# A fused RWKV, dense FFN and expert-choice MoE kernel: one-hot products for the first expert's newest rows, all second products of the last dense block held, an early start of the routing search, and one raw place kept free

## The chip, the core and the metric

The kernel runs on one core of one Trainium2 chip. The metric is device time in microseconds (us), the median of several executions. TensorE (PE) does the matmuls, VectorE (DVE) and ScalarE (ACT) work on tiles, GpSimd (POOL) and SyncE (SP) mostly issue DMAs.

## What is computed

Three parts follow one another, and the third is what matters here:

```python
x = attention(r, k, v, w, u)          # 4 x 768 tokens, 8 heads of 48: x is 3072 x 384
h = x @ w_in                          # 384 -> 2048
x = (h * sigmoid(1.702 * h)) @ w_out  # 2048 -> 384
logits = x @ w_gate                   # 8 experts
order = argsort(-logits.flatten())    # greedy: best (token, expert) pair first,
...                                   # an expert takes cap = 384 tokens, a token goes to one expert
for e in range(8):
    mask = assigned == e
    out[mask] = maximum(x[mask] @ w1[e], 0) @ w2[e]   # 384 -> 1024 -> 384
```

All of it is float32. The dense and expert weights and their inputs are split into a high and a low part (`fp32r`), so that one float32 product is three passes: high by high, high by low, low by high.

## The kernel before

**Tokens.** 3072 tokens are 24 tiles of 128 rows. Eight dense blocks of three tiles (384 tokens) run one after the other. In a block a column `f` (128 of the 2048 hidden units) has a first product `g1` (9 matmuls of 128x384, line 1207), a GELU on ACT with a split by ACT and DVE, and a second product `g2` (three `part`s of 3 matmuls, line 1235, one per tile). The result of a tile goes by ACT (line 1350) into a `cva` tile `x2` and by a DMA of ACT's queue (line 1353) to DRAM as `x2d`.

**The last block.** The routing must know all logits, so the last block makes its logits straight from the hidden columns (`thin_logits`, line 1479, two matmuls per column). Its second products are only needed later. `NIN = 2` columns are multiplied at once, the other 14 are held: 12 (`NHOLD`) in places of the ring `hold`, two in the tiles `gh`. Their 42 `part`s are the list `parts_left`. They are multiplied, tile by tile, while DVE and PE run the search of the first expert.

**Routing.** `Router.route` finds, per expert, which tokens it takes. `best()` takes each token's best open expert and makes a key; the search cuts the key in five rounds (64, 64, 64, 128, 128 steps). A round is a comparison on DVE (line 284), 24 counting matmuls (line 429), a threshold on DVE and one small matmul (line 434). Then come the expert's number `ei` (line 328), ranks, and `slots()`, which makes row numbers `idx` by 24 matmuls (line 492). `ei` lets SP read the expert's weights (line 1621, eight reads of 384 KB into `hold` places); `idx` lets POOL gather the 384 rows of `x2d` by three indirect DMAs (line 1684).

**An expert.** Each raw weight tile is split: ACT makes the high part (line 1640); the low part is made by ACT's negative copy (line 1657) with an accumulating DMA of POOL (line 1665), or, where the planner holds the DMA engines to be behind, by one DVE subtraction (line 1648). The gathered rows are transposed on PE (line 1700), split by ACT (1709) and DVE (1711), and then the eight columns run `g1` and `g2`. The search of the next experts runs between them.

**Who sets the order.** Every engine's program is fixed when the kernel is built. A planner (`Issue`) steps through a clock of its own: chains (generators) yield costs, and where the main line has nothing to do it puts filler matmuls into PE's program: narrow ones (`spin`, line 732, 128x128) or, before the first expert, wide ones (`spin_wide`, line 1783, 128x512), whose results nobody reads. On the chip an engine then runs its list in order and waits only for data.

**Between the last block and the first expert** the gathers wait for the store of the last tile, since they read all of `x2d`; the third raw read of the first expert is held back by a one-element ACT write (line 1617), the fourth by a one-element POOL write (line 1620) that stands behind the gathers.

```python
    sc.until(lambda: "ffn" in EX[0] and ("raw1", 0, 0) in wdone)   # fillers until the first expert can start
```

## Time and profile before

| | us |
|---|---|
| median of 3 executions | 822.85 (821.57 to 823.52) |
| the profiled execution, its own time | 822.38 |
| its span in the profile | 820.4 |
| last held second product ends | 550.4 |
| first matmul of the first expert starts | 564.3 |
| last matmul starts | 811.74 |

Times inside the span count from its start. The profile has one row per group of instructions; a matmul's row shows how long one matmul is in flight, which is longer than the distance at which the next one follows it.

### The profile page before, as it was taken

The numbers are of one execution on the slowest core, as the hardware profiler recorded it, in microseconds if no ns is written. First come the engines' busy times: TensorE is split into PE (matmuls) and PEld (weight loads), VectorE is DVE, ScalarE is ACT, GpSimd is POOL, SyncE is SP. The second block draws the span as 40 slices with busy tenths as digits, with TensorE's granted clock in tenths as the row PEclk, the third lists the DMA queues.
The fourth block names the chain that finished last, engine by engine and source line by source line (L and its number), as shares of the span: only waits on it lengthen the run. The fifth ranks groups of instructions, "written<-read, shape, count | busy, mean of one in ns | idle before, by whom it ended". The sixth has DMA issues, their size and how long they took to land.

```text
span 820.4 us, 17510 instructions
## 1 busy us (share of the span) xinstructions
PE 803.3 (98%) x6608; PEld 756.6 (92%) x6608; DVE 622.8 (76%) x1424; ACT 472.7 (58%) x1178; POOL 140.6 (17%) x188
## 2 busy tenths in 40 slices
PE   8999999999999999999999999999999999999995
PEld 7898999999999999999999999988898988989995
DVE  9977898879879888888879827478888887875310
ACT  5754653575676686686676644214556645576421
POOL 1001001001201101100102000003334443454211
PEclk9999999999999999999999999999999999999999
DMA  9833634412313313303313000028889899989400
GB/s 289 227 114 107 205 117 138 130 28 84 112 32 106 112 27 98 111 23 103 111 26 107 6 12 20 2 80 223 224 222 246 240 262 244 267 226 332 89 30 29
DMA packets 46068, 105.85 MB, mean 129 GB/s; under 512 B 7352, under 2 KB 13344, under 8 KB 45984
## 3 DMA queue, kind: packets, MB, share of 16 engines
q1 hardware_dynamic: 30816, 68.21, 26.5%
q0 software_dynamic: 10416, 29.50, 16.5%
q10 hardware_dynamic: 4752, 7.03, 2.4%
q8 instruction: 51, 0.84, 0.4%
q14 instruction: 33, 0.27, 0.1%
HBM read 73.60 MB, written 10.03 MB: 102 GB/s over the span
## 4 chain that ended last, share of the span: by engine, by line
PE 84%; issue 6%; DMA 5%; DVE 2%; POOL 1%; ACT 1%; SPq 0%; POOLq 0%; ACTq 0%; DVEq 0%
PE g L1207 33%; PE acc L1235 33%; PE s L1071 3%; PE s L1153 3%; PE s L429 2%; DMA cvb<-x2d,idx 2%; PE s L809 2%; PE s L1148 1%; DMA hold<-in_w 1%; DMA nat_v<-in_v 1%; PE s L1088 1%; PE s L1103 1%; PE acc L732 1%; PE s L1479 1%; POOL out L1743 1%
## 5 line engine op out<-in xcount | busy, mean ns | idle before, releaser
L1235 PE MATMUL acc<-wk,gh 128*128 128x384 f32 x1080 | 283.2, 340 | 0.1
L1235 PEld LDWEIGHTS acc<-wk,gh 128*128 128x128 f32 x1080 | 193.3, 188 | 1.6 <-issue 0.6
L1235 PE MATMUL acc<-wk,gl 128*128 128x384 f32 x540 | 181.9, 337 | 0.0
L1207 PE MATMUL g<-xha,wk 128*128 128x384 f32 x576 | 166.1, 340 | 0.0
L1207 PE MATMUL g<-xhb,wk 128*128 128x384 f32 x576 | 164.5, 339 | 0.0
L1282 ACT ACTIVATE cvb<-cvb 128x384 f32<-128x384 f32 x240 | 122.7, 517 | 8.4 <-DVE cvb L1293 7.9
L1253 ACT ACTIVATE g<-g 128x384 f32<-128x384 f32 x128 | 60.9, 476 | 101.1 <-PE g L1207 95.9
L1207 PEld LDWEIGHTS g<-xha,wk 128*128 128x128 f32 x576 | 105.4, 188 | 1.1 <-issue 0.3
L1207 PEld LDWEIGHTS g<-xhb,wk 128*128 128x128 f32 x576 | 105.1, 188 | 0.3
L1235 PEld LDWEIGHTS acc<-wk,gl 128*128 128x128 f32 x540 | 101.4, 188 | 0.0
L1207 PE MATMUL g<-xlb,wk 128*128 128x384 f32 x288 | 97.5, 339 | 0.0
L1207 PE MATMUL g<-xla,wk 128*128 128x384 f32 x288 | 97.2, 338 | 0.0
L1056 POOL TENSOR_SCALAR_AFFINE_SELECT At<-dg 128x512 f32<-128x512 f32 x38 | 35.0, 944 | 361.1 <-DVE dg L1049 273.5
L1259 DVE TENSOR_TENSOR gl<-g,gh 128x384 fp32r<-128x384 f32 x116 | 63.5, 548 | 29.1 <-ACT gh L1256 28.9
L1266 ACT ACTIVATE gh<-g 128x384 fp32r<-128x384 f32 x64 | 31.4, 491 | 88.8 <-PE g L1207 81.5
L1269 DVE SCALAR_TENSOR_TENSOR gl<-g,gh 128x384 fp32r<-128x384 f32 x64 | 35.3, 552 | 43.7 <-ACT gh L1266 43.6
L1293 DVE TENSOR_TENSOR cvb<-cva,raw 128x768 f32<-128x768 f32 x60 | 57.2, 963 | 8.5 <-ACT cva L1350 4.8
L1256 ACT ACTIVATE gh<-g 128x384 fp32r<-128x384 f32 x116 | 56.5, 487 | 6.5 <-ACT cva L1350 2.4
L1640 ACT ACTIVATE wk<-hold 128x768 fp32r<-128x768 f32 x64 | 52.9, 840 | 10.3 <-DMA hold<-in_w 10.3
L1665 POOL DMA_DIRECT2D wk<-hold x51 | 46.4, 1026 | 65.1 <-ACT wk L1657 51.9
L1207 PEld LDWEIGHTS g<-xlb,wk 128*128 128x128 f32 x288 | 54.1, 188 | 0.1
L1207 PEld LDWEIGHTS g<-xla,wk 128*128 128x128 f32 x288 | 54.1, 188 | 0.0
(282 smaller groups left out, 1264.4 us busy)
## 6 DMA issues: line engine op xcount, KB each, us to landing
hold<-in_w SPq DMA_DIRECT2D x64, 384.0 KB, 7.7
wk<-hold POOLq DMA_DIRECT2D x51, 384.0 KB, 7.6
nat_m<-in_rk SPq DMA_DIRECT2D x15, 384.0 KB, 3.1
nat_v<-in_v SPq DMA_DIRECT2D x22, 256.0 KB, 2.9
raw<-in_w_in SPq DMA_DIRECT2D x7, 768.0 KB, 4.4
raw<-in_w_out SPq DMA_DIRECT2D x7, 768.0 KB, 4.7
nat_w<-in_w SPq DMA_DIRECT2D x22, 226.2 KB, 2.9
nat_k<-in_k SPq DMA_DIRECT2D x22, 224.0 KB, 2.6
```

The lines of the kernel that those rows point to most:

```text
L1056: P.affine_select(At[s], dg[:, s::2][:, :, None].to_broadcast([128, HP, C]), pattern=[[0, HP], [1, C]], compare_op=OP.is_equal, fill=0.0, ...
L1207: T.matmul(p, self.l1(kt, f, a), (self.xh, self.xl)[b_][:, kt], start=(kt == 0 and n == 0), stop=(kt == KT - 1 and n == 2))
L1235: T.matmul(self.acc[tt], gs[a][:, tt * C:(tt + 1) * C], self.r2(f, b_), start=(f in self.cuts and n == 0), stop=(end and n == 2))
L1253: A.activation(p, p, AF.Gelu_apprx_sigmoid)
L1256: A.activation(gh, p, AF.Copy)
L1259: V.tensor_tensor(gl, p, gh.bitcast(F32), op=OP.subtract)
L1266: A.activation(gh, p, AF.Relu)
L1269: V.scalar_tensor_tensor(gl, p, 0.0, gh.bitcast(F32), op0=OP.max, op1=OP.subtract)
L1282: A.activation(t_[:, n], t_[:, n], AF.Copy, accum_out=put[n])
L1293: V.tensor_tensor(t_, x[:, None, :].to_broadcast([128, 2, Dm]), wgB[e // 4][:, (e % 4) * Dm:(e % 4 + 2) * Dm].rearrange("p (a d) -> p a d" ...
L1640: A.activation(Whi[key], raw, AF.Copy)
L1665: P.dma_start(out=Wlo[key].bitcast(F32), in_=raw, accum_op=OP.add)
```

## The change

It has five pieces.

1. **Held products.** `NIN` goes from 2 to 0 and `NHOLD` from 12 to 13: all 16 columns of the last block have their second products held (48 parts). A raw weight now needs two free places (`ok(2)`), so 12 of the 13 serve raw weights.
2. **Search begun ahead.** A chain `ahead()` runs `best()` over all 24 tiles, with the first comparison, while the last block still makes its columns; the four columns of `L` at `NC - 1::NC` hold zeros, or the logits of the block before, at that time. When the last logits are there, `best(self.redo)` does these four columns again. The three logit products share one PSUM bank and one copy.
3. **The first expert's rows of the last tile.** `slots()` numbers the rows of the last tile as row `NJ * 128`, a zero row behind `x2d` (`no_rows` writes it early). So the first expert's gathers no longer wait for the store of that tile. Its rows come from the copy `x2` that is still in SBUF: DVE makes a one-hot matrix `near` (384 slots against the ranks of the last tile), and PE adds `x2` transposed by `near`: nine float32 matmuls, line 1786. The gathered rows are added to the same PSUM by nine float32 matmuls with the identity (line 1801) in place of transposes. `all_rows()` puts the right row numbers back for the scatter.
4. **Low parts.** The DVE way of making a low part is only open from the fifth expert on (`i > 3`).
5. **First column of an expert.** The nine matmuls of column 0 are sorted: high by high, then high by low, then low by high.

```diff
-    NIN = 2
+    NIN = 0
-    NHOLD = 12
+    NHOLD = 13
...
+    def ahead():
+        while todo[0] or not late:
+            yield 0.2
...
+        router.redo = slice(NC - 1, None, NC)
...
+        yield from router.ahead()
...
         if i == 0:
-            for _ in self.best():
+            for _ in self.best(self.redo):
                 pass
...
+        if self.near is not None:
+            V.tensor_scalar(self.near, self.near, rs[:, NJ - 1:NJ], None, op0=OP.is_equal)
...
-    sc.until(lambda: todo[0] == 0)
+    sc.until(lambda: router.begun)
...
-                yield from wait("hold")
+                while not R["hold"].ok(2):
+                    yield 0.02
...
-        if sc.busy["D"] > sc.t + BEHIND:
+        if i > 3 and sc.busy["D"] > sc.t + BEHIND:
...
+        def near_rows(a):
+            for kt in range(KT):
+                T.matmul(first[a][:, kt * C:(kt + 1) * C], kept[0][0][:, kt * 128:(kt + 1) * 128],
+                         near[:, a * C:(a + 1) * C], start=kt == 0, stop=False, skip_group_check=True)
...
-            ps, done = yield from bank()
-            for kt in range(KT):
-                T.transpose(ps[:, kt * C:(kt + 1) * C], xg[a][:, kt * 128:(kt + 1) * 128], ident)
+            if i:
+                ps, done = yield from bank()
+                for kt in range(KT):
+                    T.transpose(ps[:, kt * C:(kt + 1) * C], xg[a][:, kt * 128:(kt + 1) * 128], ident)
+            else:
+                while sc.t < max(xt[a], gate[0]):
+                    yield 0.05
+                ps, done = first[a], lambda: None
+                for kt in range(KT):
+                    T.matmul(ps[:, kt * C:(kt + 1) * C], xg[a][:, kt * 128:(kt + 1) * 128], ident,
+                             start=False, stop=True, skip_group_check=True)
```

**PE, from the first gathered rows to the first expert, before** (`g` of line 1783 is a filler, `s<-oh,cvc` a counting matmul, of which only one of 24 stands here at either end, `s<-ge` the small matmul of a round; `DMASW` is a gather):

```order
L429 MATMUL s_6763<-oh,cvc 128x8
L1700 MATMUL s_6791<-ident,cvb 128x128 [waits DMASW2_49,DVE_49,PE_49]
L1700 MATMUL s_6791<-ident,cvb 128x128 x2
L1783 MATMUL g_6586<-xhb,wogp 128x512
L434 LDWEIGHTS r_ones
L434 MATMUL s_6763<-ge,r_ones 128x8 [waits DVE_49]
L1783 MATMUL g_6586<-xhb,wogp 128x512 x7
L429 LDWEIGHTS cvc [waits DVE_49]
L429 MATMUL s_6816<-oh,cvc 128x8 [waits PE_49]
```

**The same place in the change**, from the first round of the second search (`cvb` of line 1786 is `near`, `cva` the kept `x2`):

```order
L451 MATMUL s_6698<-oh,cvc 128x8
L1786 MATMUL acc_6725<-cvb,cva 128x128 [waits Activation_49]
L1786 MATMUL acc_6725<-cvb,cva 128x128 x2
L456 LDWEIGHTS r_ones
L456 MATMUL s_6698<-ge,r_ones 128x8 [waits DVE_49]
L1786 MATMUL acc_6726<-cvb,cva 128x128 x3
L1893 MATMUL g_6679<-xhb,wogp 128x512
L1786 MATMUL acc_6727<-cvb,cva 128x128 x3
L1893 MATMUL g_6679<-xhb,wogp 128x512
L451 LDWEIGHTS cvc [waits DVE_49]
```

In the whole program the wide fillers go from 40 to 10 and the narrow ones from 212 to 205; nine products with `near` and nine with the identity are new, and nine transposes are gone. The 24 matmuls of `slots()` stand before the last 22 held products and no longer behind them.

**ACT, before**, from the copy of the last tile to the split of the first expert's rows:

```order
L1350 ACTIVATE cva<-acc_5878 128x384 [waits PE_49]
L1353 DMA x2d<-cva 128x384 [waits Activation_49]
L1617 ACTIVATE hold<-r_zero 1x1
L1640 ACTIVATE wk<-hold 128x768 [waits DMAHW1_49]
L1657 ACTIVATE wk<-wk 128x768 [waits Activation_49]
...
L1709 ACTIVATE xha<-s_6733 128x3x128 [waits PE_49]
L1709 ACTIVATE xha<-s_6749 128x3x128 [waits PE_49]
L1709 ACTIVATE xha<-s_6791 128x3x128 [waits PE_49]
L1640 ACTIVATE wk<-hold 128x768 [waits DMAHW5_49,Pool_49]
L1266 ACTIVATE gh<-g_6844 128x384 [waits PE_49]
```

**and now:**

```order
L1693 ACTIVATE hold<-r_zero 1x1 [waits PE_49]
L1716 ACTIVATE wk<-hold 128x768 [waits DMAHW3_49]
L1733 ACTIVATE wk<-wk 128x768 [waits Activation_49]
...
L1716 ACTIVATE wk<-hold 128x768 [waits DMAHW5_49]
L1393 ACTIVATE cva<-acc_5887 128x384 [waits PE_49]
L1396 DMA x2d<-cva 128x384 [waits Activation_49]
L1733 ACTIVATE wk<-wk 128x768
L1814 ACTIVATE xha<-acc_6725 128x3x128 [waits PE_49]
L1814 ACTIVATE xha<-acc_6726 128x3x128 [waits PE_49]
L1716 ACTIVATE wk<-hold 128x768 [waits DMAHW6_49,Pool_49]
L1814 ACTIVATE xha<-acc_6727 128x3x128 [waits PE_49]
```

The copy of the last tile now stands behind three high parts of raw weights, and the high part of the fourth raw weight stands ahead of the split of the third tile of rows.

## Rows read from the trace of the kernel before

**Rows 1.** the page's chain that ended last, shares of the span by engine

```profile
PE 84%; issue 6%; DMA 5%; DVE 2%; POOL 1%; ACT 1%; SPq 0%; POOLq 0%; ACTq 0%; DVEq 0%
```

**Rows 2.** stages: us, busy (count) of PE, PEld, DVE, ACT, POOL, clock, DMA

```profile
550.40:564.30 13.90, 13.68 (x147) 10.60 (x147) 10.98 (x46) 7.30 (x12) 6.10 (x7) 1.00 0.70 181
564.30:812.00 247.70, 243.36 (x2108) 228.23 (x2106) 169.09 (x602) 133.03 (x217) 90.97 (x116) 1.00 0.79 209
```

**Rows 3.** timeline of the first search: start, duration, engine, line, operation, [idle before <-releaser]

```profile
525.28 0.35 DVE L247 TENSOR_REDUCE m<-L 128x24 f32<-128x192 f32 x1
525.40 3.91 PE L1235 MATMUL acc<-wk,hold 128*128 128x384 f32 x21
527.62 1.03 DVE L284 TENSOR_TENSOR cvc<-c,raw 128x768 bf16<-128x768 bf16 x2
529.15 0.76 PE L429 MATMUL s<-oh,cvc 128*128 128x8 bf16 x24
...
552.40 0.16 DVE L499 SCALAR_TENSOR_TENSOR r_tt<-so 128x3 f32<-128x3 f32 x1
552.60 0.16 DVE L501 TENSOR_TENSOR idx<-r_tt 128x3 int32<-128x3 f32 x1
```

**Rows 4.** timeline, PE between the last held product and the first expert

```profile
552.02 4.93 PE L1783 MATMUL g<-xhb,wogp 128*128 128x512 f32 x20
556.80 0.76 PE L429 MATMUL s<-oh,cvc 128*128 128x8 bf16 x24
559.86 0.76 PE L429 MATMUL s<-oh,cvc 128*128 128x8 bf16 x24
560.85 0.52 PE L1700 MATMUL s<-ident,cvb 128*128 128x128 f32 x3 [0.23 <-DMA cvb<-x2d,idx]
561.12 0.48 PE L1783 MATMUL g<-xhb,wogp 128*128 128x512 f32 x1
564.32 0.34 PE L1207 MATMUL g<-xha,wk 128*128 128x384 f32 x1
```

**Rows 5.** gathers (554.08; landing), POOL's write, five raw reads from 559.0 (landing)

```profile
554.08 1.15 POOL L1684 DMA_INDIRECT cvb<-x2d,idx  x1 [49.04 <-DVE key L255]
...
DMA to landing us min/median/max: 3.7/3.7/3.7
...
558.53 0.45 POOL L1620 MEMSET hold<- 1x1 f32 x1
...
DMA to landing us min/median/max: 4.9/8.5/9.4
```

**Rows 6.** prices on PE: one line's forms, and two stretches of the timeline

```profile
L809 PE MATMUL s<-cvc,ident x36: 483/486/590, 25.9 to 86.8; 128*128 128x384 f32 x36
...
12.53 1.00 PE L908 MATMUL s<-usel,wk 112*128 112x2 f32 x8
...
523.48 0.62 PE L732 MATMUL acc<-ident 128*128 128x128 bf16 x8
```

**Rows 7.** the page's costliest groups: sizes on ACT and DVE (mean ns of one)

```profile
L1259 DVE TENSOR_TENSOR gl<-g,gh 128x384 fp32r<-128x384 f32 x116 | 63.5, 548 | 29.1 <-ACT gh L1256 28.9
L1256 ACT ACTIVATE gh<-g 128x384 fp32r<-128x384 f32 x116 | 56.5, 487 | 6.5 <-ACT cva L1350 2.4
L1640 ACT ACTIVATE wk<-hold 128x768 fp32r<-128x768 f32 x64 | 52.9, 840 | 10.3 <-DMA hold<-in_w 10.3
```

**Rows 8.** the experts: longest wait, DVE's low parts, POOL's queue, two stretches

```profile
693.98 0.55 PE L1700 MATMUL s<-ident,cvb 128*128 128x128 f32 x3 [1.80 <-DMA cvb<-x2d,idx]
...
L1648 DVE TENSOR_TENSOR wk<-hold,wk x13: 942/957/959, 604.2 to 767.5; 128x768 fp32r<-128x768 f32 x13
...
q0 software_dynamic: 10416, 29.50, 49.1%
...
600.00:610.00 10.00, 10.00 (x85) 9.19 (x84) 9.23 (x35) 6.49 (x11) 6.19 (x9) 1.00 0.72 159
630.00:640.00 10.00, 10.00 (x100) 9.21 (x100) 8.14 (x32) 4.08 (x8) 3.85 (x6) 1.00 0.57 119
```

More of the change, by code (lines that the diff above doesn't have):

```diff
@@ L179, in __init__ @@
         self.L = pool.tile([128, NJ, E], F32, name="L")
+        self.begun, self.near = False, None
     def consts(self):
@@ L230, in numbers, with ahead @@
         return self.io[:, :n].rearrange("p (a b) -> p a b", b=2)[:, None].to_broadcast([128, k, n // 2, 2])
+    def ahead(self):
+        for _ in self.best():
+            self.S.busy["V"] = max(self.S.t, self.S.busy["V"]) + 0.42
+            yield from self.S.room("V", 0.3)
+        self.begun = True
+        yield 0.1
     def t(self, name, shape, dt=F32, bufs=2):
@@ L488, in slots @@
                 yield from self.vec(0.25, 0.4)
+        if self.near is not None:
+            V.tensor_scalar(self.near, self.near, rs[:, NJ - 1:NJ], None, op0=OP.is_equal)
+            self.near = None
+            self.S.busy["V"] += 0.35
         yield 0.2
@@ L1317 @@
     todo = [0, 0]
+    kept, sent, pairs = [], [], []
+    EX = [dict() for _ in range(E)]
     rest, stored = {}, set()
@@ L1352, in store_x2 @@
         stored.add((blk, tt))
-        nc.scalar.dma_start(x2d[j * 128:(j + 1) * 128, :], x2)
+        st = nc.scalar.dma_start(x2d[j * 128:(j + 1) * 128, :], x2)
+        if (blk, tt) == (NBLK - 1, NU - 1):
+            assert j == NJ - 1
+            kept.append((x2, sc.t, st))
+            for other in sent:
+                tc.declare_no_dep(st.ins, other.ins, reason="the first expert's gathers leave out these rows")
+        elif (blk, tt) == (NBLK - 1, NU - 2):
+            EX[0]["x2"] = sc.t + 4.0
         if blk < NBLK - 1:
@@ L1472, with no_rows @@
     parts_left = [(f, tt) for tt in range(NU) for f in range(NIN, NFS)]
+    def no_rows():
+        yield from wait("cva")
+        R["cva"].free(R["cva"].new())
+        t_ = cv.tile([128, Dm], F32, name="cva", bufs=NCVA)
+        P.memset(t_, 0.0)
+        for rows in (x2d[NT - 128:NT, :], x2d[NT:, :]):
+            nc.scalar.dma_start(rows, t_)
+        yield (("P", 0.5),)
+    def ahead():
+        while todo[0] or not late:
+            yield 0.2
+        router.late_consts(cv.tile([128, 128], BF, name="raw64", bufs=2))
+        router.Gt = [cv.tile([128, NJ // 2, 128], BF, name="cvc", bufs=NCVC) for _ in range(2)]
+        for g_ in router.Gt:
+            P.memset(g_.rearrange("p a b -> p (a b)").bitcast(F32), 0.0)
+        router.redo = slice(NC - 1, None, NC)
+        for _ in range(2):
+            yield from wait("cvb")
+            pairs.append((R["cvb"].new(), cv.tile([128, 2, Dm], F32, name="cvb", bufs=NCVB)))
+        router.near = pairs[1][1][:, 1]
+        P.iota(router.near, pattern=[[1, NB]], base=1, channel_multiplier=0,
+               allow_small_or_imprecise_dtypes=True)
+        yield (("P", 2.3),)
+        yield from router.ahead()
     def thin_logits(f, ps):
@@ L1585 @@
         spin()
-    EX = [dict() for _ in range(E)]
     scat = []
@@ L1677, in gather @@
         xg, xr, xt = [], [], []
+        rows = o["rows"]
         for a in range(NU):
             if a % 2 == 0:
-                yield from wait("cvb")
-                xr.append(R["cvb"].new())
-                pair_ = cv.tile([128, 2, Dm], F32, name="cvb", bufs=NCVB)
-            xg.append(pair_[:, a % 2])
-            P.indirect_dma_start(out=xg[a], out_offset=None, in_=x2d,
-                                 in_offset=bass.IndirectOffsetOnAxis(ap=o["idx"][:, a:a + 1], axis=0))
-            sc.busy["D"] = max(sc.busy["D"], sc.after((("P", 1.04),))) + 0.6
-            xt.append(sc.busy["D"] + (LAND if i else 1.4))
+                if i:
+                    yield from wait("cvb")
+                    pairs.append((R["cvb"].new(), cv.tile([128, 2, Dm], F32, name="cvb", bufs=NCVB)))
+                ring, pair_ = pairs.pop(0)
+                xr.append(ring)
+            xg.append(pair_[:, a % 2])
+            g_ = P.indirect_dma_start(out=xg[a], out_offset=None, in_=x2d,
+                                      in_offset=bass.IndirectOffsetOnAxis(ap=rows[:, a:a + 1], axis=0))
+            if i == 0:
+                for x in kept:
+                    tc.declare_no_dep(g_.ins, x[2].ins, reason="the first expert's gathers leave out these rows")
+                sent.append(g_)
+            sc.busy["D"] = max(sc.busy["D"], sc.after((("P", 1.04 if i else 1.43),))) + 0.6
+            xt.append(sc.busy["D"] + LAND if i else sc.t + 4.6 + 1.43 * a)
         o["sent"] = True
@@ L1712, in land @@
             done()
+            left.discard(a)
             yield (("V", 0.5),)
-            left.discard(a)
+        if i == 0:
+            for a in range(NU):
+                near_rows(a)
+                yield (("T", 0.67),)
         for a in range(NU):
```

138 lines of the change are left out of this document (88 added, 50 removed).

## Prediction

> **What bounds the kernel now.** I read the chain that ended last first. PE has 84% of it and DMA 5% [rows 1], so what PE's list holds is what time is made of, unless PE waits. Then the stages. Between the last held product (550.4) and the first expert (564.3) PE is busy for 13.68 of 13.90 us at clock 1.00, and over the experts for 243.36 of 247.70 [rows 2]. "Busy" must not be believed in the first of them: most of its 147 matmuls are wide fillers, whose results nobody reads; one row alone has 20 of them in 4.93 us [rows 4]. So the stage is mostly a wait that fillers cover. What it waits for is read in order of time: the search ends in `idx` at 552.60 + 0.16 = 552.76 [rows 3], the gathers start 1.3 us later, at 554.08, each landing 3.7 us after its issue [rows 5], and the last transposes stand at 560.85, with a wait for a gather ahead of them [rows 4]. Behind them come the split of the third tile and the first product at 564.32. So the chain is: last logits, search, `idx` and the last tile's store, gathers, split.
>
> **The change part by part.** All is set against the profiled execution, 822.38 us of its own time; the median of the runs shown is 0.47 above it.
>
> *Held products and early search.* No matmul is added: 18 products move from the last block's loop to behind it. At (3.91 - 0.34) / 20 = 0.18 us apiece [rows 3] the last logits come 3.2 us sooner, and the last held product ends where it did, as PE is full throughout. Ahead of the first count stand 10 held products and no longer 21, another 2.0 us. DVE must keep up: today it needs from 525.28 to 528.65 before that count [rows 3]; with four columns it has nine dependent small steps of about 0.20 (552.40 to 552.60 [rows 3]), so 1.8 instead of 3.4. The first count moves from 529.15 to about 524.1, 5.0 us sooner. The five rounds are unchanged, and held products fill them as before, so `idx` comes at 552.76 - 5.0 = 547.8. The early `best()` is work for DVE during the last block, where I cost it at nothing: it hides behind PE's columns. Were that cover gone, about 3.4 us of DVE work would sit there once. The comparison for `near` is one DVE step of 128x384, at most 0.55 [rows 7], put where DVE waits for the 24 `slots()` matmuls: nothing, or 0.55 on `idx`.
>
> *Gathers.* They no longer wait for the last store, so 1.3 us behind `idx`: 549.1. Today POOL is through its three gathers and one more DMA 4.5 us after the first (554.08 to 558.53 [rows 5]); so the third is issued by 553.6 at the latest and lands by 557.3.
>
> *PE between.* Thirty wide fillers go. Twenty take 4.93, so one is (4.93 - 0.40) / 19 = 0.24: minus 7.1 us. Eighteen float32 products of 128x128 come. No row has one. A float32 product shows as two records: line 809 has 18 matmuls in the program and 36 in the trace [rows 6]. Eight records with 112x128 weights and two columns advance by (1.00 - 0.25) / 7 = 0.107 [rows 6], so two records are 0.21; the far bound is four transposes, 4 x 0.09 = 0.36 (three advance from 560.85 to 561.12 [rows 4]). I take 0.22, next to the row that has the same operand type and weights: plus 4.0, between 3.8 and 6.5. Nine transposes go: minus 0.8. The sorted first column can start before the last low part of the rows is there; for it I put 0.3 us of waiting.
>
> The Trainium skill ("TensorE: Matmul & The Clock Gate", Terms) says that transpose mode is four times faster for FP32 than a plain product. By it the far bound holds, and the sum would be smaller by 18 x 0.14 = 2.5 us; line 908's row, which is a plain float32 product, speaks for the near one.
>
> A second reckoning from the order: PE's last held product ends at 550.4 plus about 0.8 for the `slots()` matmuls that now stand ahead of it. Then come 10 fillers (2.4), 18 products (4.0), three counts and three small matmuls (2.3): 8.7 us, to 559.9, and 0.3 of waiting makes 560.2. Nothing is late for it: gathered rows are wanted from about 556 to 558, `near` needs the last tile's copy by 552.6 and has it one ACT step (0.49 [rows 7]) behind 551.2, and the counts are 3.1 us apart as today (556.80, 559.86 [rows 4]). So the first product moves from 564.3 to 560.2, or 4.1; the sum of the parts, -7.1 + 4.0 - 0.8 + 0.3, says 3.6. Both stand on the same prices, and the gap between them is the waits that today's stage has.
>
> *Experts.* Seven narrow fillers fewer, at (0.62 - 0.22) / 7 = 0.06 [rows 6]: minus 0.4. Three of 13 low parts go from DVE (0.96 [rows 8]) to ACT and a DMA; PE has no part in it, and the raw stream begins 5 us sooner. Cost nothing, as long as the DMA engines have room; below that, a rival. `ok(2)` of 13 leaves the 12 places there were.
>
> Sum: -3.6 - 0.4 = -4.0. That is 818.4 for a profiled execution and **818.8** for the median. By the second reckoning it is 818.3.
>
> **The rivals.** A measurement of this kernel can tell about 0.2% (1.6 us) from no change.
>
> *The experts gain too.* They have 4.3 us without a matmul [rows 2], one wait of 1.80 for a gather among them [rows 8]. Raw weights and gathers move 5 us, the products only 4. If half to four fifths of these waits go, 816.7 to 815.3. Against it: DMAs in the middle are paced by free places, not by their start.
>
> *The price of float32.* At 0.36 apiece: 821.3.
>
> *The fourth raw read.* ACT now makes its high part ahead of the split of the third tile. It is issued behind POOL's write, at about 554.0. Of the five reads there the quickest landed after 4.9 and the slowest after 9.4 us [rows 5]. At 4.9 it is there at 558.9, and the split is hardly late; at 9.4 it is 563.4, and 0.84 + 0.49 + 0.55 [rows 7] more make 565.3: all is given back, 822.9. For the early end speaks that it is the first of the five, and first today too.
>
> *Slower: the DMA engines.* Place: the three low parts from 604.2 on [rows 8] that become DMAs. POOL's queue moved 29.50 MB in 49.1% of 276 us [rows 8], 4.6 us per MB, so 0.39 MB is 1.8 us, three are 5.4. If PE pays them in full, and one gather behind them as the 1.80 at 693.98: -4.0 + 7.2, 826.0. It turns slower once new waits pass 4.0 + 1.7 = 5.7 us. Against it: around the place the DMA share is 0.72 and 0.57 [rows 8], 2.8 + 4.3 = 7.1 us of room in 20.
>
> *The clock.* The fillers keep PE occupied. If PE waited without them and its clock went to the lower of its two levels (1.2 of 2.4 GHz), the 8.7 us of work would take 17.4: 827.5. Against it: both stages show 1.00, though the second holds a wait of 1.80 [rows 2, 8], and PE still has work all through. The Trainium skill (same page, Part 1) says that the throttled state is the default and that activity lifts it, and (Part 4) that transposes do not count as activity in the same way. By that, fewer fillers are a risk, and products for transposes are none; the trace so far agrees with neither part, as nothing here was throttled.
>
> That the change doesn't do what it says is excluded for PE by its list: 10 wide fillers, not 40.
>
> **How the numbers follow.** Forecast 0.66; the experts gain too 0.12; the float32 price 0.04; the fourth read 0.10; DMA 0.05; clock 0.03. The forecast's own spread is 817 to 820.5. From 815.2 to 821.6 the range takes in the first three and leaves out 0.18. Faster by over 0.2% (below 821.2): the first two, 0.78. Within it: 0.04 + 0.10 = 0.14. Slower: 0.08.
>
> **What would show it.** Right: first count near 524, `idx` near 548, first gather near 549, last held product near 551, first expert product near 560, 10 wide fillers, a product with `near` advancing 0.22; clock 1.00; experts as long as before within 2 us. Wrong: a gather or the third split arriving after PE wants it; a fourth read landing over 5 us after its issue; new PE waits between 600 and 640; a clock below 1.00.

## The result and the profile after

| | median us | runs | ratio to before, 95% interval |
|---|---|---|---|
| before | 821.57 (820.0 to 823.52) | 5 | |
| changed | 830.79 (828.64 to 831.75) | 5 | 1.0105 [1.0082, 1.0127] |

The change is slower by 8.6 us by the ratio (0.0105 x 821.57) and by 9.2 by the medians. 818.8 was forecast, and the range ended at 821.6. The profiled execution took 830.79 us with a span of 829.1, where that of before had 822.38 and 820.4. The experiments below stand in five groups, each with its own runs of the kernel before on the same chip. In two of them (E5 to E8, E17 and E18) that kernel itself took 825.6 and 824.2 us, and the profiles hold pauses of VectorE (the last section shows one) that no other group shows, so their times are compared within their group alone.

The stages of the changed kernel, as windows (us, then busy time and count of PE, PEld, DVE, ACT and POOL, granted clock, DMA share, GB/s):

```profile
552.20:561.40 9.20, 9.20 (x122) 7.89 (x120) 6.14 (x29) 3.87 (x8) 4.20 (x6) 1.00 0.84 219
561.40:820.70 259.30, 247.15 (x2100) 230.81 (x2099) 167.97 (x605) 135.62 (x219) 94.59 (x119) 0.99 0.78 203
```

The stage ahead of the first expert ends at 561.4, 2.9 us sooner than the 564.3 of [rows 2]. The experts last 259.3 us where they took 247.7, 11.6 more. -2.9 + 11.6 is 8.7, the difference of the spans. PE stands idle for 12.15 us in them, and stood for 4.34.

The front, PE's timeline of the changed kernel (start, duration, then the group and the idle time before it):

```profile
493.64 0.44 PE L1249 MATMUL g<-xhb,wk 128*128 128x384 f32 x1 [0.87 <-DVE hold L1300]
...
525.31 0.76 PE L451 MATMUL s<-oh,cvc 128*128 128x8 bf16 x24
...
555.68 0.83 PE L1786 MATMUL acc<-cvb,cva 128*128 128x128 f32 x6
556.26 0.47 PE L1893 MATMUL g<-xhb,wogp 128*128 128x512 f32 x1
...
561.41 0.79 PE L1249 MATMUL g<-xha,wk 128*128 128x384 f32 x3
```

The first count stands at 525.31 where [rows 3] had 529.15, so 3.8 of the 5.0 us forecast came. Of the 1.2 that are missing, 0.87 is the wait in the first line: PE wants a column's first product in the last block, and DVE's low part of an earlier column (line 1300) is late; it starts at 493.02, behind four steps of the block before (line 1351) and 0.23 us of waiting for ACT's high part. Six records of the `near` products advance by 0.58 us, 0.19 apiece (0.22 was taken). The rest of the search and the gathers (`idx` 548.80, first gather 550.02) keep this lead.

The experts: which waits of PE are longest from the first product on (engine and line, what it waited for, us in total, times, longest):

```profile
PE s L1795 <- DMA cvb<-x2d,idx: 7.4, 4, 3.2
PE g L1249 <- DVE q L442: 1.5, 1, 1.5
```

In the kernel before, transposes waited for a gather once, 1.80 us [rows 8]; now four times, 7.4 us. The two long ones stand at the sixth and the seventh expert:

```profile
711.88 1.07 POOL L1763 DMA_INDIRECT cvb<-x2d,idx  x1 [1.06 <-PE s L456]
...
723.08 0.98 PE L1795 MATMUL s<-ident,cvb 128*128 128x128 f32 x6 [3.17 <-DMA cvb<-x2d,idx]
...
739.25 1.49 POOL L1854 DMA_INDIRECT out<-cva,idx  x1 [2.77 <-ACT cva L1852]
740.74 0.91 POOL L1741 DMA_DIRECT2D wk<-hold  x1
741.95 1.05 POOL L1854 DMA_INDIRECT out<-cva,idx  x1 [0.27 <-DMA wk<-hold]
743.30 1.05 POOL L1763 DMA_INDIRECT cvb<-x2d,idx  x1 [0.30 <-issue]
...
752.54 0.55 PE L1795 MATMUL s<-ident,cvb 128*128 128x128 f32 x3 [3.12 <-DMA cvb<-x2d,idx]
```

The sixth expert's first gather is issued at 711.88 and lands 11.1 us later. The seventh's has its `idx` at 737.70, but stands in POOL's list behind a scatter that waits 2.77 us for ACT, an accumulating DMA and a second scatter; it is issued 5.6 us after its `idx` and lands 8.8 us after that. Windows around the two waits, same columns as above:

```profile
719.00:723.00 4.00, 0.91 (x26) 0.67 (x24) 1.21 (x5) 0.00 (x0) 0.00 (x0) 1.00 1.07 278
723.00:728.00 5.00, 4.40 (x21) 4.03 (x22) 2.78 (x13) 2.72 (x6) 0.00 (x0) 0.66 0.15 31
728.00:738.00 10.00, 10.00 (x81) 9.53 (x80) 7.82 (x35) 8.66 (x13) 3.52 (x5) 1.00 0.91 218
748.00:752.50 4.50, 1.43 (x9) 1.10 (x7) 0.56 (x1) 0.49 (x1) 1.14 (x2) 1.00 1.03 364
752.50:758.00 5.50, 5.03 (x21) 4.49 (x22) 2.63 (x4) 2.42 (x5) 3.11 (x3) 0.69 1.05 333
```

Behind each wait the granted clock is 0.66 and 0.69, a mix of the full and the lower level (2.4 and 1.2 GHz). If PE was all that counted there, this costs 5.0 x 0.34 = 1.7 and 5.5 x 0.31 = 1.7 us (an estimate; E2 tries to price it). The Trainium skill ("TensorE: Matmul & The Clock Gate", Part 1, HAM oscillation) says that a wait of PE for a DMA can throttle it again, so that the next work starts cold; these two rows agree. The 1.80 us wait of the kernel before was followed by clock 1.00.

The first wait also holds back the next search. DVE has the `ge` of a round ready at 720.08, but the small matmul that takes it stands in PE's list behind the first transposes of the sixth expert, and DVE waits 4.21 us for it:

```profile
724.18 0.23 PE L456 MATMUL s<-ge,r_ones 128*128 128x8 bf16 x1
...
724.45 0.17 DVE L458 TENSOR_REDUCE nm<-s 128x1 f32<-128x8 f32 x1 [4.21 <-PE s L456]
```

The seventh expert's `idx`, at 737.70, is 4.7 us later than before (733.00). In the kernel before, the first transposes of the sixth and seventh expert stand here:

```profile
724.02 0.49 PE L1700 MATMUL s<-ident,cvb 128*128 128x128 f32 x3
...
743.99 0.49 PE L1700 MATMUL s<-ident,cvb 128*128 128x128 f32 x3
```

So at the sixth expert the changed kernel, with its wait, is still 0.9 us ahead (723.08); at the seventh it is 8.6 us behind (752.54), and at the last matmul 8.6 behind (820.35 against 811.74). Set against the kernel before, the loss arises between these two places; the wait at the sixth expert has already used up most of the lead.

The page's list of groups and its queues show what else stands in the gathers' queue:

```profile
q0 software_dynamic: 10848, 30.68, 17.2%
...
L1741 POOL DMA_DIRECT2D wk<-hold x54 | 49.1, 1094 | 67.0 <-ACT wk L1733 59.8
```

There are 54 accumulating DMAs of 384 KB where there were 51, and 30.68 MB on POOL's queue where there were 29.50 [rows 8].

### The profile page after: what moved, and what is told of

Read it like the earlier page. It is cut to its first block, busy times and chain, and to the rows that moved or that the text cites. A ratio compares the mean times of both kernels' runs of the same rounds, so it can differ in the third digit from the quotient of the medians.

```text
span 829.1 us, 17509 instructions
## 1 busy us (share of the span) xinstructions
PE 803.4 (97%) x6598; PEld 756.8 (91%) x6598; DVE 622.1 (75%) x1437; ACT 476.4 (57%) x1181; POOL 144.6 (17%) x194
## 3 DMA queue, kind: packets, MB, share of 16 engines
q0 software_dynamic: 10848, 30.68, 17.2%
## 4 chain that ended last, share of the span: by engine, by line
PE 77%; issue 9%; DMA 7%; DVE 3%; POOL 2%; ACT 0%; POOLq 0%; ACTq 0%; SPq 0%; DVEq 0%
PE g L1249 30%; PE acc L1276 29%; DMA wk<-hold 4%; PE s L1110 3%; PE s L1192 3%; DMA cvb<-x2d,idx 2%; PE s L848 2%; PE s L451 2%; PE s L1187 1%; PE acc L771 1%; PE s L1127 1%; DMA hold<-in_w 1%; PE s L1142 1%; POOL out L1854 1%; POOL wk L1741 1%
## 5 line engine op out<-in xcount | busy, mean ns | idle before, releaser
L1741 POOL DMA_DIRECT2D wk<-hold x54 | 49.1, 1094 | 67.0 <-ACT wk L1733 59.8
L1716 ACT ACTIVATE wk<-hold 128x768 fp32r<-128x768 f32 x64 | 53.4, 839 | 11.1 <-DMA hold<-in_w 11.1
```

The source lines that it names most:

```text
L1716: A.activation(Whi[key], raw, AF.Copy)
L1741: P.dma_start(out=Wlo[key].bitcast(F32), in_=raw, accum_op=OP.add)
```

## The experiments

The working table, from the traces. "Experts" runs from the first product to the last matmul; "fillers" are the narrow ones among the experts at the 0.06 us of the prediction; "clock" is (1 - granted clock) x stretch, an estimate of what the lower clock costs.

| kernel | first product | experts | PE waits | fillers | clock | time, us |
|---|---|---|---|---|---|---|
| before | 564.32 | 247.42 | 4.1 | 34: 2.0 | 0 | 822.38 |
| changed | 561.41 | 258.94 | 12.1 | 27: 1.6 | 3.4 | 830.79 |
| E10, rule off | 561.41 | 250.77 | 4.8 | 69: 4.1 | 0 | 822.31 |
| E11, and no fillers | 561.05 | 251.66 | 5.5 | 0 | 5.2 | 822.83 |
| E13, rule off, later numbers | 561.58 | 249.21 | 5.3 | 29: 1.7 | 0 | 821.04 |

Of the 11.5 us by which the changed kernel's experts are longer, waits are 8.0, the clock 3.4 and fillers -0.4; 0.5 is left. The theory at first (A): the rule `i > 3` puts more accumulating DMAs on POOL's queue, and the gathers come late behind them. Rivals: a gather is slow by itself (theory B in E1), the planner puts the transposes too early into PE's list (theory D in E3), or holding all products brings the loss. Theories that come later have further letters in the expectations.

**E1: five accumulating DMAs left out**, those around the sixth and seventh expert.

```diff
-        P.dma_start(out=Wlo[key].bitcast(F32), in_=raw, accum_op=OP.add)
+        lows[0] += 1
+        if not 38 <= lows[0] <= 42:
+            P.dma_start(out=Wlo[key].bitcast(F32), in_=raw, accum_op=OP.add)
```

> Leaves out five accumulating DMAs of 384 KB, those that stand on POOL's queue between the fifth and the sixth expert's gathers (702.95 to 709.96 in the changed kernel); the low parts of five weight tiles are then wrong. All lists are otherwise the same. Theory A (the DMA engines are behind: the sixth expert's gather, issued at 711.88, landed after 11.1 us because it waits its turn behind these transfers): it lands 4 to 6 us sooner, the wait of 3.17 us ahead of its transposes at 723.08 goes, and the clock stays at 1.00 there: 5 us less than the changed kernel, about 826. Theory B (the gather is slow of itself, or waits for something on POOL): the landing stays near 11 us and the time within 1 us of the changed kernel's.

825.33 us, 1.0044 [1.003, 1.0058], 5.5 below the changed kernel. The sixth expert's gathers, by the view of the tile, in the changed kernel:

```profile
DMA to landing us min/median/max: 9.4/10.2/11.1
```

and in E1, where PE no longer waits for them:

```profile
DMA to landing us min/median/max: 3.1/3.4/4.0
```

POOL's queue between 711 and 723 (packets, MB, share of 16 engines) in the changed kernel:

```profile
q0 software_dynamic: 953, 2.69, 97.7%
```

and in E1:

```profile
q0 software_dynamic: 337, 0.98, 35.9%
```

The queue was full for all of these 12 us, and a gather of 128 rows stood in it. The Trainium skill ("DMA: Bandwidth & Descriptors", Two DMAs through the same engine are not ordered) says that within one queue of one DMA engine descriptors start in order; a gather that lands after 11.1 us behind earlier DMAs of its queue and after 3.1 without five of them agrees. Theory A has its link for the sixth expert, and theory B falls. With that wait gone the seventh `idx` comes at 733.36 and not at 737.70, so the wait was what held the search. The seventh's own wait (2.8) stayed.

**E2: 48 narrow fillers ahead of the first transposes of experts 6 and 7**, to price the clock alone.

```diff
+            if i in (5, 6) and a == 0:
+                spin(48)
```

> 48 narrow filler matmuls, some 2.9 us, stand on PE directly ahead of the first transposes of the sixth and of the seventh expert, where PE waits 3.17 and 3.12 us in the changed kernel; nothing else moves. Theory C (part of the loss is the clock: after each of these waits the granted clock is 0.59 to 0.82 for about 4 us): the clock stays at 1.00 and the time falls by 3 to 4.5 us, to about 827, though PE gets no work done sooner. Rival (the lower clock is an effect that PE's idle time causes but that costs nothing, since PE is behind data anyway): within 0.5 us of the changed kernel, or up to 1 us slower.

830.13 us, 1.0097 [1.0074, 1.0121]: 0.7 less, not the 3 to 4.5 forecast. In its profile the clock from 720 to 760 is 1.00 and the experts take 256.3 us, 2.6 less than in the changed kernel. But from 630 to 640 it is 0.83, behind two short waits, and from 30 to 60 it was 0.95; the first product stands at 564.30, 2.9 us later. So the clock could be lifted at the place, and the time did not show it: inconclusive as a price, and the 3.4 us of the table stay an estimate.

**E3: transposes of experts 6 to 8 planned 3.5 us later.**

```diff
-            xt.append(sc.busy["D"] + LAND if i else sc.t + 4.6 + 1.43 * a)
+            xt.append(sc.busy["D"] + LAND + (3.5 if i > 4 else 0.0) if i else sc.t + 4.6 + 1.43 * a)
```

> The planner is told that gathered rows of the sixth expert and later land 3.5 us later than it holds now, so it puts the transposes of the sixth expert 16 matmuls (2.8 us) later into PE's list, of the seventh 36 and of the eighth 53. Theory D (the rows land at a time that the DMA engines set, and the change only made PE come to them too soon, as the search ran ahead): the waits of 3.17 and 3.12 us go or fall under 1 us, the clock stays at 1.00: 6 to 10 us less, 821 to 825. Rival (the rows are what bounds, whatever the order): PE waits elsewhere, for the split rows at the first columns of those experts, and the time stays above 828.

825.3 us, 1.0036 [1.0022, 1.0051]. The sixth expert's wait is gone, since PE's list has other work there, though its gathers still land after 8.9 to 10.6 us; the seventh's wait (3.16) is as in the changed kernel, so only half of the forecast came. The time falls by 5.5 us, as much as in E1, where the gathers themselves were sooner. Theory D is true as far as it goes: a late gather costs because PE's list is fixed with the transposes early. The edit moves other work too: 52 accumulating DMAs are left of 54.

**E4: the rule `i > 3` taken away, all else of the change kept.**

```diff
-        if i > 3 and sc.busy["D"] > sc.t + BEHIND:
+        if sc.busy["D"] > sc.t + BEHIND:
```

> Undoes one piece of the change: DVE may again make low parts for every expert. Theory E (the three low parts that went from DVE to accumulating DMAs put the DMA engines behind): the waits for gathers in the experts fall back to about those of the kernel before (4.5 us in all, from 12), and the time to 820 or 821. Rival (the order that the planner comes to from another start is what costs, and any start may do): waits for gathers stand elsewhere, and the time lies anywhere from 818 to 831.

822.5 us, 1.0007 [0.9993, 1.002]. PE waits in the experts fall to 4.6 us, as forecast, and accumulating DMAs from 54 to 46. The time is 1.5 above the upper end of what was expected: level with before, though the first product stands 3 us sooner. Holding all products falls as the cause of the loss, and a second question opens: where do these 3 us go?

**E5: the rule alone, in the kernel before.**

```diff
-        if sc.busy["D"] > sc.t + BEHIND:
+        if i > 3 and sc.busy["D"] > sc.t + BEHIND:
```

> The kernel before with one piece of the change alone: DVE makes low parts only from the fifth expert on. It issues 53 accumulating DMAs where the kernel before has 51, the changed one 54 and the changed one with DVE open 46. Theory A (the time follows the load on the DMA engines, some 1.8 us for each accumulating DMA): 2 to 4 us slower than the kernel before, 823 to 826, with new waits for gathers of 2 us or more. Rival (the piece alone is harmless; it costs only together with the earlier search): within 1 us of the kernel before.

834.89 us, 1.0113 [1.0083, 1.0142]. Slower in its group by 9.3 us, but its longest waits are not gathers:

```profile
PE s L434 <- DVE ge L431: 8.7, 6, 2.1
PE s L1700 <- DMA cvb<-x2d,idx: 1.9, 1, 1.9
```

PE waits six times, 8.7 us in all, for a DVE step of 0.17. Those are the pauses told of above (the last section shows one), so E5 does not show what the rule does to the kernel before.

**E6 and E11: the rule off, and no fillers in the experts** (the same kernel, in two groups).

```diff
-    sc.spin = spin
+    sc.spin = None
```

> The changed kernel with DVE open for all low parts, and the 69 narrow fillers of the experts left out; no other instruction moves. That kernel with its fillers spent 250.1 us from the first expert's first product to the last matmul, the kernel before 247.4, at about the same idle time (4.6 and 4.1 us), with 35 fillers more. Theory F (the fillers are what ate the gain of the earlier start, 35 x 0.06 = 2.1 us): PE's list gets 69 x 0.06 = 4 us shorter, and the time falls by 2 to 4 us, to 819 or 820. Rival (the fillers only fill time in which PE would wait for weights or rows): the same idle time stands in their place, and the time stays within 0.7 us of 822.5; with a lower clock behind the new waits it is 1 to 3 us slower.

E6: 830.58 us, 1.0059 [1.004, 1.0078], with 7.4 us of waits for `ge` in its profile.

> The same without the 69 fillers of the experts, beside it. Theory F (the fillers ate the gain): 2 to 4 us less than with them. Rival (PE would wait for weights and rows in their place): within 0.7 us, or slower where the clock falls.

E11: 822.65 us, 1.0013 [1.0001, 1.0024], with 0.5 us of them. Beside it in its group the changed kernel again, E9:

> The changed kernel itself, so that it and the next three share one chip and the same runs of the kernel before. All theories: 1.0 to 1.1% slower than the kernel before.

E9: 830.88 us, 1.0111 [1.0089, 1.0133], with the two long waits at the same places (2.83 and 3.02 us); and the rule off with its fillers, E10:

> The changed kernel with DVE open for all low parts, once more beside the changed kernel. Theory E (the accumulating DMAs, 54 against 46, are the loss): 0.7 to 1.1% less than the changed kernel. Rival (what it showed belongs to the chip that it ran on): within 0.3% of the changed kernel.

E10: 823.06 us, 1.0018 [1.0001, 1.0034]. The rule costs 830.88 - 823.06 = 7.8 us in one group on one chip. Of accumulating DMAs E10 has

```profile
L1741 POOL DMA_DIRECT2D wk<-hold x46 | 41.5, 974 | 77.6 <-ACT wk L1733 57.8
```

where the changed kernel has 54. Taking E10's fillers away changes nothing in the time (823.06 and 822.65), and the windows say why. E10:

```profile
640.00:680.00 40.00, 38.82 (x413) 35.02 (x412) 35.41 (x150) 21.47 (x34) 14.34 (x18) 1.00 0.89 235
```

E11:

```profile
640.00:680.00 40.00, 37.56 (x352) 33.94 (x352) 33.37 (x141) 19.77 (x32) 13.55 (x17) 0.87 0.89 239
```

Without fillers PE waits instead (1.14 us for one comparison) and its clock is 0.87 there, 40 x 0.13 = 5.2 us; with them 49 of E10's 69 fillers stand there, 2.9 us. E10's second `idx` is level with that of the kernel before (581.94 against 581.90), but its fourth is 5.0 us later (657.63 against 652.59), and these 49 fillers stand behind it, from 660.5 to 667. So the place waits for the fourth search either way; what makes that search late is not shown.

**E7: the rule off, but the planner lets DVE make a low part only when the DMA engines are 2.0 us behind, not 1.0.**

```diff
-    BEHIND = 1.0
+    BEHIND = 2.0
...
-        if i > 3 and sc.busy["D"] > sc.t + BEHIND:
+        if sc.busy["D"] > sc.t + BEHIND:
```

> The changed kernel, DVE open for all experts, but only when the planner holds the DMA engines to be 2.0 us behind and no longer 1.0: 54 accumulating DMAs and 10 low parts on DVE, as in the changed kernel, but in another order (the scatters stand ahead of or among the accumulating DMAs otherwise, the transposes of the fifth and sixth expert 20 and 32 matmuls later). Theory A (the number of accumulating DMAs sets the loss): 827 to 831. Theory D (the place of the transposes in PE's list against the landing of the rows sets it): 819 to 824, with no wait for rows over 1.5 us.

831.16 us, 1.0068 [1.0044, 1.0092], with 4.7 us of waits for `ge`: from the time nothing follows. Its waits for gathers do say something: with 54 accumulating DMAs, as many as in the changed kernel, PE waits for a gather once, 1.3 us, and not 7.4. That is the sign of theory D. The number of these DMAs alone does not make the waits.

**E8: the rule off and two products not held** (`NIN = 2` as before).

```diff
-    NIN = 0
+    NIN = 2
...
+            if f2 < NIN:
+                for tt in range(NU):
+                    last.part(f2, tt)
```

> The changed kernel with DVE open, and two columns of the last block multiplied at once as before: 18 second products stand again ahead of the last logits. The changed kernel's logits came 1.9 us sooner where 3.2 were reckoned, with a wait of 0.87 at 493.64 for DVE's low part of an early column. Theory G (that wait is the price of holding all products, as PE comes to the column too soon for DVE): the wait goes here, the first count comes 1.5 to 2.3 us later, the first expert's first product 1 to 2 us later than with all held, the time 0.5 to 2 us longer than 822.5. Rival (the wait comes from the search begun ahead): it stays, and the first product comes 3 us later.

834.01 us, 1.01 [1.0076, 1.0123], 3.4 above E6, which also lacks the fillers of the experts; both have pauses, so the front alone is read. In its profile the wait at 493 for DVE's low part is gone. The clock of 30 to 60 was 0.94 in this execution, and the same matmuls of the last block stand 2.2 us later than in E6; with that taken off, the first count is at 527.2 (E6: 524.93) and the first product at 563.2 (561.07). So holding all products is worth about 2 us at the front, even with its wait (0.87 in the changed kernel, 0.6 in E6).

**E12: as E11, and every fifth accumulating DMA left out** (9 of 46), to see whether the DMA engines hold the experts even without the rule.

```diff
+        if lows[0] % 5:
+            P.dma_start(out=Wlo[key].bitcast(F32), in_=raw, accum_op=OP.add)
```

> The same without fillers, and every fifth accumulating DMA left out, 9 of 46, so that nine low parts are wrong; no other instruction moves. Theory H (the DMA engines hold the experts, so an earlier first product is given back in waits as long as the same bytes have to come): 9 x 1.8 = 16 us of work for the DMA engines less, PE's waits in the experts fall under 4 us, and the time falls 3 to 6 us below the kernel with all of them, to 816 to 819 where the kernel before takes 821.5. Rival (what holds the experts is DVE, ACT or the search): the time falls by less than 1.5 us.

822.91 us, 1.0015 [1.0001, 1.003]: the same as E11. Nine accumulating DMAs fewer bring nothing, so their load does not hold what is left. Theory H falls.

So the search was followed. DVE's timeline of the changed kernel, in the fourth round of the second search (`u`, `c` and `cvc` are the round's steps; line 1310 is the low part of the first expert's first column):

```profile
562.99 0.21 DVE L470 SCALAR_TENSOR_TENSOR u<-v,hf 128x48 f32<-128x48 f32 x1
564.39 0.56 DVE L1310 SCALAR_TENSOR_TENSOR gl<-g,gh 128x384 fp32r<-128x384 f32 x1 [1.20 <-ACT gh L1307]
564.87 0.18 DVE L428 CAST c<-u 128x48 bf16<-128x48 f32 x1
565.08 1.97 DVE L306 TENSOR_TENSOR cvc<-c,raw 128x768 bf16<-128x768 bf16 x4
```

DVE has `u` at 563.2, but its next step in the list is the first column's low part, which waits 1.20 us for ACT. In the kernel before, the copy and the comparison came first:

```profile
565.48 0.21 DVE L448 SCALAR_TENSOR_TENSOR u<-v,hf 128x48 f32<-128x48 f32 x1
565.72 0.19 DVE L406 CAST c<-u 128x48 bf16<-128x48 f32 x1
565.94 1.96 DVE L284 TENSOR_TENSOR cvc<-c,raw 128x768 bf16<-128x768 bf16 x4
```

The fourth count thus stands at 567.41 where it was 567.91: of the 3.7 us that the second search led at its first round (553.10 against 556.80) 0.5 are left. The second expert's `idx` is at 582.06, and was at 581.90: the search's lead, and with it that of the gathers, is gone there. Whether DVE's order is what took it is tried by E13 and E15.

**E13: the rule off, and `all_rows()` moved behind the first expert's second product**, which takes five small steps out of DVE's list in the second search.

```diff
-        if i == 0:
-            router.all_rows(o)
...
+        if i == 0:
+            while at[0] < 2:
+                yield 0.1
+            router.all_rows(o)
```

> The changed kernel with DVE open for all low parts, and the first expert's rows renumbered for the scatter only when its third column begins; with that the planner puts the comparison of the second search's fourth round ahead of the low part of the first column. 45 narrow fillers in place of 85, 15 low parts on DVE. Theory J (the gain of the front was lost in DVE's list of the second search): the fourth count comes 2 us or more sooner than 567.2, the second expert's idx sooner than 581.9 by 1 to 3, and the time is 818 to 820.5. Rival (something later holds the experts: the search of the fourth expert, DVE or the DMA engines): the second expert's idx is sooner, but the time stays within 1 us of 823.

820.91 us, 0.9993 [0.9983, 1.0003]: level with before, and 2.4 us under the rule off alone (each against the median of before in its group: -1.0 here, +1.3 for E10; the two intervals just touch). DVE's list now has the copy and the comparison ahead of the low part:

```profile
563.10 0.21 DVE L470 SCALAR_TENSOR_TENSOR u<-v,hf 128x48 f32<-128x48 f32 x1
563.34 0.19 DVE L428 CAST c<-u 128x48 bf16<-128x48 f32 x1
563.56 1.97 DVE L306 TENSOR_TENSOR cvc<-c,raw 128x768 bf16<-128x768 bf16 x4
565.45 0.55 DVE L1310 SCALAR_TENSOR_TENSOR gl<-g,gh 128x384 fp32r<-128x384 f32 x1
```

The fourth count is at 566.69 and the second `idx` at 580.89, 1.0 sooner than before; 29 fillers stand in the experts, not 69. The count came 0.5 us sooner than in E10 where 2 or more were expected, and the time lies just above the expected range. More than five steps moved: there are 49 accumulating DMAs against E10's 46. So the gain of 2.4 us is measured, and its cause is not singled out.

**E14: the same with the rule kept.**

> The changed kernel with the later renumbering alone; its rule for low parts (DVE from the fifth expert on) stays; 52 accumulating DMAs. Theory J with theory A: the second search gains as in the run before, but the rule still costs: 824 to 829. Rival (the second search is the whole loss, and the rule was harmless with it in order): 818 to 821.

826.83 us, 1.0066 [1.005, 1.0083]. The rule costs 5.9 us here too, though the order around it is another.

**E15: as E10, with the comparison of that fourth round drawn ahead of the low part** by leaving out one pause of the planner.

```diff
-                yield (("T", 0.1), ("V", 0.9))
+                if self.halves == 2:
+                    self.S.busy["V"] = max(self.S.t, self.S.busy["V"]) + 0.9
+                else:
+                    yield (("T", 0.1), ("V", 0.9))
```

> The changed kernel with DVE open, and the comparison of the second search's fourth round issued directly behind the step ahead of it; the renumbering stays in front of it. 61 fillers, 15 low parts on DVE. Theory J: the fourth count comes 1.2 to 2.5 us sooner, the time is 819 to 822. Rival: within 1 us of 823.

826.59 us, 1.0062 [1.0044, 1.008]: missed. DVE compares at 563.47 now, 2.1 us sooner than in E10 (565.53), but the fourth count came only 0.2 sooner, at 567.07 against 567.24: PE's list has products of the first expert and two fillers up to it, and PE runs them without a wait from 563.83 on. So DVE's order alone does not hold that count, and theory J is not shown. Elsewhere the fixed lists fell differently (49 accumulating DMAs, not 46): the seventh expert's gather is issued 4.1 us behind its `idx`, PE waits 4.32 us for it, and the clock from 720 to 760 is 0.91. An edit meant for 563 brought a wait of 4 us at 750, with the rule off.

**E16: the rule from the fourth expert on** (`i > 2`).

> The changed kernel with its rule eased by one expert (DVE makes low parts from the fourth on): 52 accumulating DMAs, 45 fillers; the second search is as in the changed kernel. Theory A: with two accumulating DMAs fewer it lies between the changed kernel and the one with DVE open, 825 to 830. Theory J: the second search's fourth count stays at 567.4.

828.23 us, 1.0089 [1.0071, 1.0108]; PE waits 5.3 us for gathers, 3.3 of it at one place. The fourth count is at 568.55, later than expected. Its interval overlaps that of the changed kernel in E9 ([1.0089, 1.0133]): one expert more with the DVE way open is no cure.

**E17 and E18: E13 with another order of the first column's products, with and without fillers.**

```diff
-                steps.sort(key=lambda x: x[1])
+                steps.sort(key=lambda x: (0, 2, 1)[x[1]] if at[0] else x[1])
```

> The kernel with DVE open and later renumbering; in the first column of the second expert and later the three products that need the low part of the rows stand last, behind the three with the low weights. Nothing else moves. Theory K (PE waits there for the split, with nothing else ahead): the wait of 1.70 at 629.06 falls by 3 x 0.17 = 0.5 us, other waits for the split at an expert's start by up to 0.3: 0.5 to 1.0 us less than 820.9, about 820.2. Rival (what is gained there is lost at the next wait): 820.9.

> The same without the 29 fillers of the experts. If they stand on the path: 29 x 0.06 = 1.7 us less than with them. Rival (they cover waits and keep the clock): within 0.5 us, or 1 to 3 us more where the granted clock falls below 1.00 behind a wait.

831.13 us, 1.0076 [1.0049, 1.0103], and 830.95 us, 1.0076 [1.005, 1.0103]. E17's waits:

```profile
PE s L456 <- DVE ge L453: 6.5, 6, 1.9
PE s L1795 <- DMA cvb<-x2d,idx: 1.9, 3, 1.5
```

The 6.5 us are the pauses again, and the order of the products stays open. Without its 29 fillers the same kernel takes as long, as the rival of E18 has it.

## Why the prediction was wrong

**Held products, early search.** Right in kind. The first count was to move by 5.0 us and moved by 3.8. The step "I cost it at nothing: it hides behind PE's columns" was said of `best()`; what was not covered was a low part of a held column, which stands on DVE behind steps of the block before and for which PE waited 0.87 us. With two columns multiplied at once this wait is gone (E8). The five rounds and the gathers then went as forecast.

**PE between.** Right. 10 wide fillers, 0.19 us per product with `near` against 0.22, clock 1.00, first product at 561.41 against the 560.2 of the second reckoning, of which the 1.2 stood at the first count already. The far price (0.36) fell. The Trainium skill's figure beside it ("TensorE: Matmul & The Clock Gate", Terms: transpose mode four times faster for FP32) is not borne out here: 0.19 is about two of the transposes of [rows 4], at 0.09 apiece. The fourth raw read was in time: the third split stood at 560.48 and no product waited for it.

**Experts.** This step failed: "Three of 13 low parts go from DVE (0.96) to ACT and a DMA; PE has no part in it ... Cost nothing, as long as the DMA engines have room", and the sentence that the experts last as before within 2 us. They last 11.5 us longer, to the last matmul. The rule costs 7.8 us (E9 and E10) and 5.9 (E14 and E13). The room was read from 600 to 640, by a DMA share of 0.72 and 0.57 in two windows of ten. The two windows between them, which the prediction left out, had none:

```profile
610.00:620.00 10.00, 10.00 (x101) 9.42 (x100) 8.48 (x36) 5.63 (x9) 3.32 (x4) 1.00 1.02 333
620.00:630.00 10.00, 9.73 (x98) 8.72 (x98) 8.66 (x28) 8.06 (x13) 5.21 (x7) 1.00 1.08 239
```

And it had to be read where a gather stands in the queue: the profile of before had such a place, the 1.80 us at 693.98 in [rows 8], and its share from 640 to 700 is 1.00:

```profile
640.00:700.00 60.00, 57.78 (x574) 52.59 (x573) 50.39 (x207) 35.12 (x55) 23.18 (x29) 1.00 1.00 261
```

The three low parts do not stand there themselves. E1 shows for the sixth expert that the DMAs that do stand there set the landing, and the traces of the changed kernel and of E1 that PE's wait for it held back the search of the seventh. E9 against E10 shows that the rule costs 7.8 us and that PE's waits for gathers fall without it, from 6.6 us to 1.1. How the rule leads to them is shown only in part: it is not the number of accumulating DMAs alone, since E7 has 54 and 1.3 us of such waits, and E15 has 49, without the rule, and 4.3. E3 speaks for the order: there a later place of the transposes in PE's list took the sixth expert's wait away. Where the gathers, the transposes and the DMAs fall against each other in the fixed lists thus counts too, and no run separates this from the load. The rival "Slower: the DMA engines" had part of the mechanism, a gather behind such DMAs, and 7.2 us of new cost where the rule costs 7.8; but its place was 600 to 640, its chance 0.05, and it held no clock: the rival on the clock looked at fillers and not at a wait for a DMA.

**And the gain at the front.** The forecast let all of it through to the end. Without the rule none of it arrives (E4, E10): the second search has given its lead back by 582. That this is due to DVE's list, where the rounds stand between the first expert's splits and `all_rows()`, was argued and not borne out by E15. In the table E10's experts are 3.4 us longer than before, of which 0.6 are waits and 2.1 fillers; most of its fillers stand where PE would wait behind the fourth search (E11). "The experts gain too" asked what else could move and did not ask what could hold them.

**The other pieces.** Without the two free places (`ok(2)`) the program is the same, instruction by instruction. Without the sort only the order of the nine products of an expert's first column changes on PE; no run was made of it, so its worth is not shown.

**What stays open.** By what steps the rule brings the late gathers. What makes the second and the fourth search of E10 give up their lead: not the load of the accumulating DMAs (E12), and not DVE's order at one place (E15). Whether the new wait at the seventh expert in E15 has a cause of its own or is only where the lists happened to fall. What the rule costs in the kernel before (E5), and the order of E17. No version beat the kernel before: E13 is 0.07% under it, with an interval that holds 1.

## What to carry to other kernels

A stage made shorter counted here only as far as the chain that paces the next stage came sooner as well: follow it (here search, `idx`, gather) until the program ends or the lead is gone. Before work is put on a DMA queue, look for the transfers of that queue that an engine waits for, and read the queue's share there, over the whole stretch, not where the work is issued. Where a search and the work that it feeds share an engine's list, a wait of the one holds back the other, as at 723 here. Where lists are fixed by a planner, a small move may bring a wait at a far place, so price a piece by undoing it alone and look at all long waits, not only at the one it was meant for.

## What the runs showed of the hardware that was not expected

- The landing of a gather of 128 rows took from 3.1 to 11.1 us at the same place, by what stood in POOL's queue (E1).
- The clock after a wait was not told by the wait's length alone. After 3.17 and 3.12 us it was 0.66 and 0.69; after 1.80 in the kernel before it was 1.00; in E11, where no single wait from 640 to 680 was above 1.14 us but PE's idle time there was 2.4, it was 0.87. What the Trainium skill says of waits for a DMA ("TensorE: Matmul & The Clock Gate", Part 1, HAM oscillation) fits the first two; the last is not explained here.
- In two groups DVE started a step of 0.17 us about 2 us after its input, in the line below with "remote" as the releaser. The same kernel had 7.4 us of such waits as E6 and 0.5 as E11, and 830.58 and 822.65 us. E17, where the counts of the round had ended by 635.83:

```profile
638.31 0.17 DVE L453 TENSOR_SCALAR ge<-s 128x8 bf16<-128x8 f32 x1 [2.17 <-remote]
638.53 0.17 PE L456 MATMUL s<-ge,r_ones 128*128 128x8 bf16 x1 [1.89 <-DVE ge L453]
```

What a pause waits for is not in these traces.
